# Two bf16 values as one 4-byte element: all transposes of a retention and mixing kernel on TensorE, none on the DMA

## Chip, cores and metric

One core of one Trainium2 chip. The metric is the device time of one execution in microseconds (us), as the median of several runs. "The span" is the length of one profiled execution; where the time and the span of the same run are both known, the time is in most runs about 1.7 us longer. "The clock" is the share of its full rate that TensorE was granted. A run more than 1.5% above the fastest of the same kernel is called slow; medians and ranges hold all runs, ratios the fast ones alone.

## The reference, cut to what matters

```python
# q, k, v: (4, 8, 768, 64) fp32;  attention with a decaying state
state = gamma * state + k_t (outer) v_t          # per head
y_t   = scale * q_t @ state
# x = y as (4, 768, 512); then the mixing layer
theta = x @ w_theta
y = w_tok_r @ (x * cos(theta)) + w_tok_i @ (x * sin(theta))   # over tokens
u = x + y
out = u + max(u @ w_ch, 0)
```

The kernel does it in chunks of 128 tokens: 24 chunks of attention, and 24 rows (blocks of 128 tokens) of the mixing layer. In each product of TensorE here the summed index lies on the partitions, so k and q of each chunk, the attention result x, the rows of u and the token weights must each be turned by 128x128 blocks in bf16.

## The kernel before

The parts that the change touches. `att_*` are the steps of a chunk, `moe_*` those of a row.

```python
N_DMA = (B - 1) * nT + 1     # chunks from 19 on are turned by DMA
M_DMA = (B - 2) * nT         # rows from 12 on are turned by DMA
...
def att_prep(n):
    kqb = work.tile([P, 2, dm], BF, name="kqb", bufs=5)
    kb, qb = kqb[:, 0, :], kqb[:, 1, :]          # k and q side by side
    ...                                          # GpSimd casts and scales into them
def att_T(n):
    kq_ps = psum.tile([P, 2 * NP, P], BF, name="kq_ps", tag="tr", bufs=2)
    for i, src in enumerate((s["kb"], s["qb"])):
        for j in range(NP):                      # 8 transposes of 2-byte elements
            nc.tensor.transpose(kq_ps[:, i * NP + j, :], src[:, j * P:(j + 1) * P], ident)
    nc.vector.tensor_copy(kqT, kq_ps)            # contiguous copy out of PSUM
def att_T_dma(n):
    nc.sync.dma_start_transpose(out=kqT, in_=s["kqb"].rearrange("p a d -> p (a d)"))
...
def moe_last(m):             # the last row, in two halves
    ...
    moe_U_dma(m - 1)
    prods(0)
    moe_O(m - 2)
    prods(1)
    flip(0)
    moe_O(m - 1)
    flip(1)
    ...
# one slot of the main loop, in TensorE's order (cut)
    if n is not None and nT < n < N_DMA:       att_T(n)
    ...
    if U_at.get(s_ - 1, 0) >= M_DMA:           moe_O(U_at[s_ - 1])   # DMA row: a slot later
    ...
    if U_at.get(s_, M_DMA) < M_DMA:            moe_U(U_at[s_])
    ...
    if 1 < U_at.get(s_, M_DMA) < M_DMA:        moe_O(U_at[s_])
```

## Time and profile before

| | before |
|---|---|
| time, first runs | 182.69 us (182.03 to 184.78, 3 runs) |
| time beside the later calls, medians | 182.41 to 183.72 us |
| span of the profiled run, clock | 181.8 us, 1.00 in nearly every slice |
| TensorE busy | 157.7 us, 87% |
| VectorE, ScalarE, GpSimd busy | 104.8, 74.7, 79.9 us |

First, two of the three kinds of DMA transposes, and the output of whole rows, in the list of DMA issues (what, engine, count, for the output the size, median microseconds from issue to landing):

```profile
uT<-u SPq DMA_TRANSPOSE x11, 2.4
kqT<-kqb SPq DMA_TRANSPOSE x5, 3.8
out_dram<-ot SPq DMA_DIRECT2D x23, 256.0 KB, 2.2
```

Issuing one takes SyncE 1.2 us (median of the 11 of u).

Second, the end of the chain of waits in order of time (start, length, what):

```profile
171.92 0.76 PE y_ps L348 x7
172.67 3.02 DMA uT<-u
...
175.73 0.39 PE o_ps L310
...
177.35 0.41 PE o_ps L374 x2
```

The last row's y products start at 171.92 us. The chain then leaves TensorE for the DMA transpose of row 22, whose landing releases the o products at 175.73 us; TensorE itself waited only 0.2 us for it. TensorE is done at 177.76 us, and the output has landed by 181.8.

### The profile page before, as it was taken

The numbers are of one execution on the slowest core, as the hardware profiler recorded it, in microseconds if no ns is written. First come the engines' busy times: TensorE is split into PE (matmuls) and PEld (weight loads), VectorE is DVE, ScalarE is ACT, GpSimd is POOL, SyncE is SP. The second block draws the span as 40 slices with busy tenths as digits, with TensorE's granted clock in tenths as the row PEclk, the third lists the DMA queues.
The fourth block names the chain that finished last, engine by engine and source line by source line (L and its number), as shares of the span: only waits on it lengthen the run. The fifth ranks groups of instructions, "written<-read, shape, count | busy, mean of one in ns | idle before, by whom it ended". The sixth has DMA issues, their size and how long they took to land.

```text
span 181.8 us, 3528 instructions
## 1 busy us (share of the span) xinstructions
PE 157.7 (87%) x1367; PEld 90.7 (50%) x1392; DVE 104.8 (58%) x146; ACT 74.7 (41%) x140; POOL 79.9 (44%) x104
## 2 busy tenths in 40 slices
PE   0567987897764999999999999999999999999991
PEld 0344655553542655656565565455545544444560
DVE  1264794716822777878676877765645744434442
ACT  4053764821429535647554363356345332200010
POOL 4648677869075768865777847250000000000000
PEclk9999999999999999999999999999999999999997
DMA  6999999999998999999999989984483333334433
GB/s 128 222 316 218 224 276 259 294 288 231 227 259 180 260 243 225 222 272 271 223 228 251 266 208 233 263 151 115 119 112 102 103 97 90 104 93 110 132 105 117
DMA packets 95265, 35.63 MB, mean 196 GB/s; under 512 B 89488, under 2 KB 89744, under 8 KB 95248
## 3 DMA queue, kind: packets, MB, share of 16 engines
q1 hardware_dynamic: 95104, 35.27, 86.4%
q8 instruction: 11, 0.18, 0.5%
q10 hardware_dynamic: 144, 0.13, 0.2%
q14 instruction: 6, 0.05, 0.1%
HBM read 25.69 MB, written 6.29 MB: 176 GB/s over the span
## 4 chain that ended last, share of the span: by engine, by line
PE 62%; SPq 18%; DMA 12%; issue 2%; POOL 2%; DVE 1%; DVEq 0%
PE y_ps L282 27%; SPq L80 15%; PE o_ps L310 11%; PE th_ps L253 8%; DMA kf<-in_k_dram 4%; DMA qf<-in_q_dram 3%; PE yT_ps L214 3%; DMA wtok<-in_moe_w_tok_r_dram 3%; PE at_ps L185 3%; PE kq_ps L165 3%; PE st_ps L222 2%; SPq L94 2%; DMA uT<-u 2%; PE yT_ps L203 2%; PE x_ps L250 1%
## 5 line engine op out<-in xcount | busy, mean ns | idle before, releaser
L282 PE MATMUL y_ps<-z,wti 128*128 128x512 bf16 x137 | 51.9, 379 | 1.6 <-ACT wti L332 0.9
L282 PE MATMUL y_ps<-z,wtr 128*128 128x512 bf16 x125 | 47.4, 379 | 0.7 <-DVE u L287 0.3
L189 DVE TENSOR_TENSOR at<-at_ps,mask 128x1024 bf16<-128x1024 f32 x24 | 29.3, 1220 | 8.9 <-PE at_ps L185 8.8
L258 ACT ACTIVATE cs<-th_ps,halfpi 128x512 bf16<-128x512 f32 x24 | 16.5, 688 | 38.0 <-PE th_ps L253 34.1
L154 POOL TENSOR_TENSOR kqb<-qf,qsc 128x512 bf16<-128x512 f32 x24 | 25.7, 1071 | 11.3 <-DMA qf<-in_q_dram 11.1
L156 POOL TENSOR_TENSOR vb<-vf,vsc 128x512 bf16<-128x512 f32 x24 | 25.9, 1081 | 7.0 <-DMA vf<-in_v_dram 5.8
L264 DVE TENSOR_TENSOR z<-cs,x_sb 128x1024 bf16<-128x1024 bf16 x24 | 19.6, 818 | 14.2 <-ACT cs L259 14.2
L168 DVE COPY kqT<-kq_ps 128x1024 bf16<-128x1024 bf16 x19 | 13.1, 691 | 24.6 <-PE kq_ps L165 24.4
L253 PE MATMUL th_ps<-wth,xT 128*128 128x512 bf16 x89 | 24.4, 387 | 2.4 <-DVE wth L395 1.9
L153 POOL CAST kqb<-kf 128x512 bf16<-128x512 f32 x24 | 16.0, 667 | 19.9 <-DMA kf<-in_k_dram 14.1
L310 PE MATMUL o_ps<-wch,uT 128*128 128x512 bf16 x88 | 23.1, 379 | 0.4 <-DMA uT<-u 0.2
L165 PE MATMUL kq_ps<-ident,kqb 128*128 128x128 bf16 x152 | 13.6, 234 | 11.1 <-POOL kqb L153 7.0
L287 DVE TENSOR_TENSOR u<-y_ps,x_sb 128x512 bf16<-128x512 f32 x23 | 15.8, 690 | 11.9 <-PE y_ps L282 11.9
L313 DVE SCALAR_TENSOR_TENSOR ot<-o_ps,u 128x512 f32<-128x512 f32 x23 | 15.9, 692 | 10.7 <-PE o_ps L310 10.7
L231 ACT CAST xT<-yT_ps 128x512 bf16<-128x512 f32 x24 | 14.1, 586 | 19.4 <-PE yT_ps L214 18.1
L282 PEld LDWEIGHTS <-wti 128*128 128x128 bf16 x138 | 13.5, 98 | 15.4 <-issue 1.9
L282 PEld LDWEIGHTS <-wtr 128*128 128x128 bf16 x138 | 13.5, 98 | 13.5
L165 PEld LDWEIGHTS <-kqb 128*128 128x128 bf16 x152 | 10.6, 104 | 16.5 <-POOL kqb L153 7.9
L259 ACT ACTIVATE cs<-th_ps,zerob 128x512 bf16<-128x512 f32 x24 | 16.3, 681 | 0.0
L236 ACT CAST stbd<-st_ps 64x256 bf16<-64x256 f32 x40 | 14.7, 366 | 0.5
L310 PEld LDWEIGHTS <-uT 128*128 128x128 bf16 x92 | 8.8, 98 | 10.3 <-DMA uT<-u 0.4
L253 PEld LDWEIGHTS <-xT 128*128 128x128 bf16 x96 | 8.8, 100 | 9.2 <-issue 2.6
(51 smaller groups left out, 147.3 us busy)
## 6 DMA issues: line engine op xcount, KB each, us to landing
kf<-in_k_dram SPq DMA_DIRECT2D x24, 256.0 KB, 4.9
qf<-in_q_dram SPq DMA_DIRECT2D x24, 256.0 KB, 5.0
vf<-in_v_dram SPq DMA_DIRECT2D x24, 256.0 KB, 5.3
out_dram<-ot SPq DMA_DIRECT2D x23, 256.0 KB, 2.2
wtok<-in_moe_w_tok_r_dram SPq DMA_DIRECT2D x6, 384.0 KB, 5.3
wtok<-in_moe_w_tok_i_dram SPq DMA_DIRECT2D x6, 384.0 KB, 5.9
w<-in_moe_w_theta_dram SPq DMA_DIRECT2D x1, 1024.0 KB, 6.7
w<-in_moe_w_ch_dram SPq DMA_DIRECT2D x1, 1024.0 KB, 7.8
```

Source lines behind the costliest of these rows:

```text
L80: nc.sync.dma_start(out=t, in_=src[b, :, c * P:(c + 1) * P, :].rearrange("h s d -> s h d"))
L153: nc.gpsimd.tensor_copy(kb.rearrange(r3, h=H), raw[n, "kf"])
L154: nc.gpsimd.tensor_mul(qb.rearrange(r3, h=H), raw[n, "qf"], _bcast_last(qsc[:, c], D))
L156: nc.gpsimd.tensor_mul(vb.rearrange(r3, h=H), raw[n, "vf"], _bcast_last(vsc[:, c], D))
L165: nc.tensor.transpose(kq_ps[:, i * NP + j, :], src[:, j * P:(j + 1) * P], ident)
L189: nc.vector.tensor_mul(at.rearrange("p a j t -> p (a j) t"), at_ps.rearrange("p a j t -> p (a j) t"), _bcast_mid(mask, H))
L253: nc.tensor.matmul(th_ps, s["xT"][:, j, :], wth[:, j, :], start=(j == 0), stop=(j == NP - 1))
L258: nc.scalar.activation(cs[:, 0, :], th_ps, AF.Sin, bias=halfpi, scale=1.0)
L259: nc.scalar.activation(cs[:, 1, :], th_ps, AF.Sin, bias=zerob, scale=1.0)
L264: nc.vector.tensor_mul(zs[b][:, c], st[n]["cs"], _bcast_mid(xs[b][:, c, :], 2))
L282: nc.tensor.matmul(y_ps, wT[r][:, s0, t0 * P:(t0 + 1) * P], zs[b][:, s0, r, :], start=(s0 == 0 and r == 0), stop=(s0 == nT - 1 and r == 1))
L310: nc.tensor.matmul(o_ps, mo[m]["uT"][:, j, :], wch[:, j, :], start=(j == 0), stop=(j == nD - 1))
```

## The change

The intent: a 4-byte element holds two bf16 values, so a transpose of 128x128 4-byte elements turns two blocks at once. With half the instructions, TensorE takes over all transposes, also those of the DMA. k and q are stored interleaved, and the copy of VectorE out of PSUM takes them apart with a step of two elements. For u and the token weights the pairs are left in, and the reader of the turned block (a weight load with a step of two) picks its half. For x, the theta products read the unturned block with a step of two, and the features of the turned one come out in another order; the weights of theta are put into that order too, and the last sum undoes it. The core of the diff (the same pattern for x, u and the token weights, and the reordered weights, are cut):

```diff
-    N_DMA = (B - 1) * nT + 1
-    M_DMA = (B - 2) * nT
...
-    ident = const.tile([P, P], BF)
+    ident = const.tile([P, P], FT)
...
-        kqb = work.tile([P, 2, dm], BF, name="kqb", bufs=5)
-        kb, qb = kqb[:, 0, :], kqb[:, 1, :]
+        kqb = work.tile([P, dm, 2], BF, name="kqb", bufs=5)
+        kb, qb = kqb[:, :, 0], kqb[:, :, 1]
...
+        kq_ps = psum.tile([P, NP, P], FT, name="kq_ps", tag="tr", bufs=2)
+        for j in range(NP):
+            nc.tensor.transpose(kq_ps[:, j, :],
+                                s["kqb"][:, j * P:(j + 1) * P, :].rearrange(
+                                    "p c i -> p (c i)").bitcast(FT), ident)
+        kqT = work.tile([P, 2, NP, P], BF, name="kqT", bufs=4)
+        nc.vector.tensor_copy(kqT.rearrange("p i j t -> p i (j t)"),
+                              kq_ps.rearrange("p j t -> p (j t)").bitcast(BF)
+                                  .rearrange("p (c i) -> p i c", i=2))
-    def att_T_dma(n):                      # and att_X_dma, moe_U_dma
...
     def moe_last(m):
-        moe_U_dma(m - 1)
+        moe_U(m - 1)
         prods(0)
         moe_O(m - 2)
...
-        if n is not None and nT < n < N_DMA:
+        if n is not None and n > nT:
             att_T(n)
...
-        if U_at.get(s_ - 1, 0) >= M_DMA:
-            moe_O(U_at[s_ - 1])
...
-        if 1 < U_at.get(s_, M_DMA) < M_DMA:
+        if U_at.get(s_, 0) > 1:
             moe_O(U_at[s_])
```

More of the change, by code (lines that the diff above doesn't have):

```diff
@@ L141 @@
     wch = const.tile([P, nD, dm], BF)
-    wT = [const.tile([P, nT, S], BF, name="wtr"), const.tile([P, nT, S], BF, name="wti")]
+    wT = [const.tile([P, nT, nT // 2, P, 2], BF, name="wtr"),
+          const.tile([P, nT, nT // 2, P, 2], BF, name="wti")]
     st = {}
@@ L161, in att_T @@
         s = st[n]
-        kq_ps = psum.tile([P, 2 * NP, P], BF, name="kq_ps", tag="tr", bufs=2)
-        for i, src in enumerate((s["kb"], s["qb"])):
-            for j in range(NP):
-                nc.tensor.transpose(kq_ps[:, i * NP + j, :],
-                                    src[:, j * P:(j + 1) * P], ident)
-        kqT = work.tile([P, 2 * NP, P], BF, name="kqT", bufs=4)
-        nc.vector.tensor_copy(kqT, kq_ps)
-        s["kqT"] = kqT
-    def att_T_dma(n):
-        s = st[n]
-        kqT = work.tile([P, 2 * NP, P], BF, name="kqT", bufs=4)
-        nc.sync.dma_start_transpose(
-            out=kqT, in_=s["kqb"].rearrange("p a d -> p (a d)"))
-        s["kqT"] = kqT
+        kq_ps = psum.tile([P, NP, P], FT, name="kq_ps", tag="tr", bufs=2)
[5 more added lines that the diff above has]
+        nc.vector.tensor_copy(kqT.rearrange("p i j t -> p i (j t)"),
+                              kq_ps.rearrange("p j t -> p (j t)").bitcast(BF).rearrange("p (c i) -> p i c", i=2))
+        s["kT"] = [kqT[:, 0, j, :] for j in range(NP)]
+        s["qT"] = [kqT[:, 1, j, :] for j in range(NP)]
     def att_A(n):
         s = st[n]
-        kqT = s["kqT"]
         at_ps = psum.tile([P, 2, NP, P], FT, name="at_ps", tag="at", bufs=1)
@@ L184, in att_A @@
                 rows = slice(par * D, (par + 1) * D)
-                nc.tensor.matmul(at_ps[:, par, j, :], kqT[rows, j, :],
-                                 kqT[rows, NP + j, :], start=(j == 0),
+                nc.tensor.matmul(at_ps[:, par, j, :], s["kT"][j][rows],
+                                 s["qT"][j][rows], start=(j == 0),
                                  stop=(j == NP - 1), skip_group_check=True)
@@ L203, in att_Yinter @@
                 nc.tensor.matmul(s["yT_ps"][:, j, :], stbd[c % 2][:, j, :],
-                                 s["kqT"][:, NP + j, :], start=(j == 0), stop=False,
+                                 s["qT"][j], start=(j == 0), stop=False,
                                  skip_group_check=True)
@@ L229, in att_Y @@
             zs[b] = big.tile([P, nT, 2, dm], BF, name="z")
-        xT = work.tile([P, NP, P], BF, name="xT", bufs=3)
-        nc.scalar.copy(xT, yT_ps)
+        xT = work.tile([P, NP // 2, P, 2], BF, name="xT", bufs=3)
+        nc.scalar.copy(xT.rearrange("p a t b -> p a b t"),
+                       yT_ps.rearrange("p (b a) t -> p a b t", b=2))
         s["xT"] = xT
@@ L236, in att_Y @@
                 nc.scalar.copy(stbd[(c + 1) % 2][sl, :, sl], st_ps[b][sl, :, sl])
-    def att_X_dma(n):
-        b, c = divmod(n, nT)
-        nc.sync.dma_start_transpose(
-            out=xs[b][:, c, :].rearrange("p (j e) -> p j e", j=NP),
-            in_=st[n]["xT"].rearrange("p j t -> p (j t)"))
     def att_X(n):
@@ L246, in att_X @@
         s = st[n]
-        if n < N_DMA:
-            x_ps = psum.tile([P, NP, P], BF, name="x_ps", tag="tr", bufs=2)
-            for j in range(NP):
-                nc.tensor.transpose(x_ps[:, j, :], s["xT"][:, j, :], ident)
+        x_ps = psum.tile([P, NP // 2, P], FT, name="x_ps", tag="tr", bufs=2)
+        for a in range(NP // 2):
+            nc.tensor.transpose(x_ps[:, a, :],
+                                s["xT"][:, a].rearrange(
+                                    "p t i -> p (t i)").bitcast(FT), ident)
         th_ps = psum.tile([P, dm], FT, name="th_ps", tag="acc", bufs=2)
         for j in range(NP):
-            nc.tensor.matmul(th_ps, s["xT"][:, j, :], wth[:, j, :], start=(j == 0),
-                             stop=(j == NP - 1))
-        if n < N_DMA:
-            nc.vector.tensor_copy(xs[b][:, c, :], x_ps.rearrange("p j e -> p (j e)"))
+            nc.tensor.matmul(th_ps, s["xT"][:, j % 2, :, j // 2], wth[:, j, :],
+                             start=(j == 0), stop=(j == NP - 1))
+        nc.vector.tensor_copy(xs[b][:, c, :],
+                              x_ps.rearrange("p a e -> p (a e)").bitcast(BF))
         cs = work.tile([P, 2, dm], BF, name="cs", bufs=2)
@@ L281, in moe_M @@
             for r in range(2):
-                nc.tensor.matmul(y_ps, wT[r][:, s0, t0 * P:(t0 + 1) * P],
+                nc.tensor.matmul(y_ps, wT[r][:, t0, s0 % (nT // 2), :, s0 // (nT // 2)],
                                  zs[b][:, s0, r, :], start=(s0 == 0 and r == 0),
@@ L290, in moe_U @@
     def moe_U(m):
-        u_ps = psum.tile([P, nD, P], BF, name="u_ps", tag="tr", bufs=2)
-        for j in range(nD):
-            nc.tensor.transpose(u_ps[:, j, :], mo[m]["u"][:, j * P:(j + 1) * P], ident)
-        uT = work.tile([P, nD, P], BF, name="uT", bufs=3)
-        nc.scalar.copy(uT, u_ps)
-        mo[m]["uT"] = uT
-    def moe_U_dma(m):
-        uT = work.tile([P, nD, P], BF, name="uT", bufs=3)
-        nc.sync.dma_start_transpose(out=uT, in_=mo[m]["u"])
-        mo[m]["uT"] = uT
+        u_ps = psum.tile([P, nD // 2, P], FT, name="u_ps", tag="tr", bufs=2)
+        for a in range(nD // 2):
+            nc.tensor.transpose(u_ps[:, a, :],
+                                mo[m]["u"][:, 2 * a * P:2 * (a + 1) * P].bitcast(FT),
+                                ident)
+        uT = work.tile([P, nD // 2, P, 2], BF, name="uT", bufs=3)
+        nc.scalar.copy(uT.rearrange("p a t i -> p (a t i)"),
+                       u_ps.rearrange("p a t -> p (a t)").bitcast(BF))
+        mo[m]["uT"] = [uT[:, j % 2, :, j // 2] for j in range(nD)]
     def moe_O(m):
         b, t0 = divmod(m, nT)
-        if m >= M_DMA:
-            o_ps = psum.tile([P, dm], FT, name="o_ps", tag="tr", bufs=2)
-        else:
-            o_ps = psum.tile([P, dm], FT, name="o_ps", tag="acc", bufs=2)
+        o_ps = psum.tile([P, dm], FT, name="o_ps", tag="acc", bufs=2)
         for j in range(nD):
-            nc.tensor.matmul(o_ps, mo[m]["uT"][:, j, :], wch[:, j, :], start=(j == 0),
+            nc.tensor.matmul(o_ps, mo[m]["uT"][j], wch[:, j, :], start=(j == 0),
                              stop=(j == nD - 1))
         ot = work.tile([P, dm], FT, name="ot", bufs=4)
-        nc.vector.scalar_tensor_tensor(ot, o_ps, 0.0, mo[m]["u"], ALU.max, ALU.add)
+        nc.vector.scalar_tensor_tensor(
+            ot.rearrange("p (b r) -> p b r", b=2),
+            o_ps.rearrange("p (b r) -> p b r", b=2), 0.0,
+            mo[m]["u"].rearrange("p (r b) -> p b r", b=2),
+            ALU.max, ALU.add)
         nc.sync.dma_start(out=out[b, t0 * P:(t0 + 1) * P, :], in_=ot)
@@ L320, in w_cast @@
             row = work.tile([P, S], BF, name="wrow", bufs=3)
-            nc.gpsimd.tensor_copy(row, wdma[r, t0])
+            nc.gpsimd.tensor_copy(
+                row.rearrange("p (i b) -> p b i", b=2),
+                wdma[r, t0].rearrange("p (b i) -> p b i", b=2))
             wrow[r, t0] = row
@@ L325, in w_tok @@
         for r in range(2):
-            w_ps = psum.tile([P, nT, P], BF, name="w_ps", tag="tr", bufs=2)
-            for s0 in range(nT):
-                nc.tensor.transpose(w_ps[:, s0, :],
-                                    wrow[r, t0][:, s0 * P:(s0 + 1) * P], ident)
-            dst = wT[r][:, :, t0 * P:(t0 + 1) * P]
+            w_ps = psum.tile([P, nT // 2, P], FT, name="w_ps", tag="tr", bufs=2)
+            for a in range(nT // 2):
+                nc.tensor.transpose(
+                    w_ps[:, a, :],
+                    wrow[r, t0][:, 2 * a * P:2 * (a + 1) * P].bitcast(FT), ident)
+            dst = wT[r][:, t0].rearrange("p a t b -> p (a t b)")
+            src = w_ps.rearrange("p a t -> p (a t)").bitcast(BF)
             if r:
-                nc.scalar.copy(dst, w_ps)
+                nc.scalar.copy(dst, src)
             else:
-                nc.vector.tensor_copy(dst, w_ps)
+                nc.vector.tensor_copy(dst, src)
     def moe_last(m):
@@ L342, in moe_last @@
         u = work.tile([P, dm], BF, name="u", bufs=4)
-        uT = work.tile([P, nD, P], BF, name="uT", bufs=3)
+        uT = work.tile([P, nD // 2, P, 2], BF, name="uT", bufs=3)
         def prods(e):
@@ L347, in prods @@
                 for r in range(2):
-                    nc.tensor.matmul(y_ps[e], wT[r][:, s0, t0 * P:(t0 + 1) * P],
+                    nc.tensor.matmul(y_ps[e], wT[r][:, t0, s0 % (nT // 2), :, s0 // (nT // 2)],
                                      zs[b][:, s0, r, e * hw:(e + 1) * hw],
@@ L355, in flip @@
         def flip(e):
-            u_ps = psum.tile([P, 2, P], BF, name="u_ps", tag="tr", bufs=2)
-            for j in range(2):
-                jj = 2 * e + j
-                nc.tensor.transpose(u_ps[:, j, :], u[:, jj * P:(jj + 1) * P], ident)
-            nc.scalar.copy(uT[:, 2 * e:2 * e + 2, :], u_ps)
-        moe_U_dma(m - 1)
+            u_ps = psum.tile([P, P], FT, name="u_ps", tag="tr", bufs=2)
+            nc.tensor.transpose(u_ps, u[:, e * hw:(e + 1) * hw].bitcast(FT), ident)
+            nc.scalar.copy(uT[:, e].rearrange("p t i -> p (t i)"), u_ps.bitcast(BF))
+        moe_U(m - 1)
         prods(0)
@@ L370, in moe_last @@
                 psum.tile([P, hw], FT, name="o_ps", tag="acc", bufs=2)]
-        for js in ((0, 1), (2, 3)):
+        for js in ((0, 2), (1, 3)):
             for e in range(2):
                 for j in js:
-                    nc.tensor.matmul(o_ps[e], uT[:, j, :],
+                    nc.tensor.matmul(o_ps[e], uT[:, j % 2, :, j // 2],
                                      wch[:, j, e * hw:(e + 1) * hw], start=(j == 0),
@@ L378, in moe_last @@
             ot = work.tile([P, hw], FT, name="oh", bufs=2)
-            nc.vector.scalar_tensor_tensor(ot, o_ps[e], 0.0, u[:, e * hw:(e + 1) * hw],
-                                           ALU.max, ALU.add)
+            nc.vector.scalar_tensor_tensor(
+                ot, o_ps[e], 0.0, u.rearrange("p (r b) -> p b r", b=2)[:, e],
+                ALU.max, ALU.add)
             (nc.sync, nc.scalar)[e].dma_start(
@@ L394 @@
         if n == 1:
-            nc.vector.tensor_copy(wth, wdma["th"])
+            nc.vector.tensor_copy(
+                wth[:, :nD // 2].rearrange("p d (r b) -> p d b r", b=2),
+                wdma["th"][:, :nD // 2].rearrange("p d (b r) -> p d b r", b=2))
+            nc.scalar.copy(
+                wth[:, nD // 2:].rearrange("p d (r b) -> p d b r", b=2),
+                wdma["th"][:, nD // 2:].rearrange("p d (b r) -> p d b r", b=2))
         if n > 0:
@@ L445 @@
             load_chunk(n + 5)
-        if U_at.get(s_, 0) >= M_DMA:
-            moe_U_dma(U_at[s_])
-        if n is not None and nT < n < N_DMA:
+        if n is not None and n > nT:
             att_T(n)
@@ L458 @@
             w_cast(3 + s_ // 2)
-        if s_ + 1 in n_of and n_of[s_ + 1] < N_DMA:
+        if s_ + 1 in n_of:
             att_prep(n_of[s_ + 1])
-        if s_ + 2 in n_of and n_of[s_ + 2] >= N_DMA:
-            att_prep(n_of[s_ + 2])
-            att_T_dma(n_of[s_ + 2])
         if s_ in (1, 3, 5):
             w_tok(3 + s_ // 2)
-        if U_at.get(s_ - 1, 0) >= M_DMA:
-            moe_O(U_at[s_ - 1])
         if s_ - 1 in n_of:
             att_Yinter(n_of[s_ - 1])
-        if U_at.get(s_, M_DMA) < M_DMA:
+        if s_ in U_at:
             moe_U(U_at[s_])
@@ L475 @@
             att_Y(n_of[s_ - 1])
-            if n_of[s_ - 1] >= N_DMA:
-                att_X_dma(n_of[s_ - 1])
         if s_ == 2:
```

## The prediction

> **What bounds the kernel now.** I read the page first (slices, chain), then the table of windows, the chain in order of time, and the groups by form. The slices of the page show two stages:
>
> ```profile
> PE   0567987897764999999999999999999999999991
> DMA  6999999999998999999999989984483333334433
> q1 hardware_dynamic: 95104, 35.27, 86.4%
> PE 62%; SPq 18%; DMA 12%; issue 2%; POOL 2%; DVE 1%; DVEq 0%
> ```
>
> In the first 13 slices (to about 58 us) the DMA engines are full and TensorE is not; from there to the end TensorE is at 9 tenths in every slice. The chain splits in the same place: 30% of the span is DMA and its queue, all of it at the start, and 62% is TensorE. In order of time it crosses over here, and then runs through TensorE slot by slot:
>
> ```profile
> 51.51 6.18 DMA qf<-in_q_dram
> 57.76 1.05 POOL kqb L154
> 58.86 0.41 PE kq_ps L165 x4
> 59.29 0.04 DVE kqT L168
> 59.33 0.57 issue
> 59.90 0.68 DVE z L264
> 60.59 0.69 DVE u L287
> 61.28 0.47 DVE wtr L334
> 61.80 0.38 PE u_ps L293 x4
> ...
> 98.42 0.45 PE kq_ps L165 x8
> 98.87 1.29 PE y_ps L282 x6
> 100.16 0.22 PE yT_ps L203 x4
> 100.39 0.22 PE u_ps L293 x4
> ```
>
> The reader is to see that a load's landing releases the kq transposes at 58.86 us, that after a short stretch on VectorE everything on the chain is TensorE back to back, and that eight kq transposes cost 0.45 us, four u transposes 0.22 us: 56 ns each from start to start. (The 219 to 234 ns in the groups is the length of one, with its pipeline; what a packed stage pays is the 56 ns.) One full slot, 98.42 to 104.86 us, is 6.44 us, and the pieces of the chain sum to it: kq 0.45, y 2.53, carried y 0.22, u 0.22, at 0.33, yT 0.34, state 0.33, o 0.86, x 0.22, theta 0.86, with about 0.06 between. So after 58.9 us, time is the sum of what TensorE is given. Loads are not behind there: the chunk whose kq transposes start at 98.4 us was ready on GpSimd at 89 us, though the one used at 66.0 us was ready at 62.5 us, so early on there are only some 3.5 us to spare.
>
> The rows that the sum needs:
>
> ```profile
> L165 PE MATMUL kq_ps<-ident,kqb 128*128 128x128 bf16 x152 | 13.6, 234 | 11.1 <-POOL kqb L153 7.0 <-POOL kqb L154 4.1
> L165 PEld LDWEIGHTS <-kqb 128*128 128x128 bf16 x152 | 10.6, 104 | 16.5 <-POOL kqb L153 7.9 <-POOL kqb L154 5.0 <-issue 0.5
> L168 DVE COPY kqT<-kq_ps 128x1024 bf16<-128x1024 bf16 x19 | 13.1, 691 | 24.6 <-PE kq_ps L165 24.4
> L189 DVE TENSOR_TENSOR at<-at_ps,mask 128x1024 bf16<-128x1024 f32 x24 | 29.3, 1220 | 8.9 <-PE at_ps L185 8.8
> ```
>
> **What the Trainium skill says.** "TensorE: Matmul & The Clock Gate", Terms (xbus row), has a transpose mode that is "4× faster for FP32". If a 4-byte matmul otherwise takes four passes, the 128 columns of a 4-byte transpose stream as fast as 2-byte ones. The same page, Weight-path perf modes, says fast weight load is on for 128 weights whose type is not FP32, and its section LDWEIGHTS gives columns divided by 1.2, so 107 ns for 128. In this kernel the data to be turned is the weight operand (the second row above), so that path is used by every transpose. The trace agrees for 2 bytes (56 ns apart, so weights load inside that) and has not one 4-byte operand on TensorE: the cost of the new transpose is in no row. "VectorE: DVE Perf Modes", What auto-detection actually checks, gives the mode with two elements per cycle only to 16-bit operands of step 1. The trace agrees: 1024 bf16 contiguous from PSUM take 691 ns, 1024 elements in fp32 take 1220 ns. "GPSIMD Engine Reference", Performance pitfalls, warns of reads with a step over 8 bytes; the new steps are 4 bytes and on the write side, which no row shows.
>
> **The change part by part**, after 58.9 us, where TensorE's sum is the time.
>
> Removed. Transposes of 2 bytes on TensorE: kq of 10 chunks x 8 = 80, x of 12 chunks x 4 = 48, u of 10 rows x 4 and the last row's 4 = 44, token weights 2 x 12 = 24. Sum 196, at 0.0556 us: 10.9 us. Removed too are 21 DMA transposes (5 kqT, 5 x, 11 uT). These cost the chain almost nothing: TensorE waited for uT 0.22 us in all, in the tail.
>
> Added. The remaining work with half the instructions, but also the share that the DMA did: kq of 15 chunks x 4 = 60, x of 17 x 2 = 34, u of 21 rows x 2 and the last's 2 = 44, weights 2 x 6 = 12. Sum 150, each costing t. So the TensorE sum changes by 150 t - 10.9 us. It breaks even at t = 73 ns. A normal slot goes from 6.44 to 6.44 - 0.89 + 8t; a late slot, whose transposes were on the DMA, gets 8t on top.
>
> What t is, is the whole question:
> - 56 ns, if the stream is one column per cycle and the weights load behind the previous stream: -2.5 us.
> - 107 ns, if the 4-byte weight load without the fast path is the limit: 150 x 0.107 = 16.1, so +5.2 us.
> - 160 ns, if load and stream no longer overlap (107 + 53): +13.1 us.
> - 213 ns, if four passes are made after all (4 x 53): +21.1 us.
>
> Moved. The kq copy must read with step 2, so it drops to one element per cycle: 691 to about 1220 ns, the time of the at product. That is +0.53 us per slot and five more copies, plus five x copies of 0.41 us. Per slot VectorE goes from about 4.5 us (ot 0.69, x 0.41, kqT 0.69, z 0.82, at 1.22, u 0.69) to 5.0 of 6.4 us: beside TensorE, not on the path. It is on the path in one place, the VectorE stretch at 59.3 to 61.8 us: +0.5 us. ScalarE gets 11 more uT copies of 586 ns; it is idle there.
>
> The tail. The row before the last was turned by DMA while TensorE went on with the last row. Now its transposes stand first in TensorE's order and wait for the VectorE sum u (0.69 us plus 0.2 us of latency): about +0.9 us, less the 0.2 us of the wait removed, +0.7 us.
>
> The first stage: the loads and their queue bound it, and they do not change. TensorE has some 10 us idle between 10 and 57 us, so its transposes there are free at t up to about 213 ns (78 instead of 156).
>
> Strided weights (theta, o, y, state products): loads of 98 ns beside streams of 216 ns, hidden; I count nothing.
>
> Sum: 182.7 + 150 t - 10.9 + 1.2, that is 181 at 56 ns, 189 at 107, 196 at 160, 204 at 213.
>
> **The rivals.**
> (a) TensorE's sum falls and the kernel gets slightly faster. For: half the transposes, the page's phrase on FP32. Against: even then it is 2.5 us less the 1.2 us of new waits. Result 180 to 182.
> (b) The 4-byte weight load becomes the bound of each transpose, and the DMA's share comes back onto the full engine. For: the page excludes FP32 from the fast load, and the late slots were relieved on purpose. Against: weight loads of 128 rows x 64 columns, which by "TensorEngine Tiling (Array Packing)", Restrictions, have no fast path either, take 109 ns here against 98, only 11 ns more, so a slow load may still hide. Result 188 to 197.
> (c) VectorE becomes the bound, with 5.0 us in slots that shrink to 6.0. For: its copies must come just before the at product. Against: over 1 us per slot is left, and in the slot at 105 us the copy would still end some 0.3 us before the product needs it. Result 1 to 3 us on top of (a).
> (d) The DMA was slowed by its transposes, and loads get faster without them. Against: the kq transposes are issued at 110 us and later, when the last loads are going out. Worth nothing.
>
> **Range and chances.** I give t near 56 ns 0.40, near 107 ns 0.32, and 160 ns or more 0.28. The middle of that is about 187 us, between the cases rather than in one. Eight in ten: 180 to 203. Faster by 2% needs 179.0 us or less, which even (a) misses: 0.05. Within 2% (up to 186.3 us) is (a) with or without (c): 0.42. Slower: 0.53.
>
> **What would show it.** Look for eight transposes per slot of 4-byte type: their start-to-start time is t, and the stretch after about 59 us should move by 150 t - 10.9 us. The kqT copy should read about 1220 ns. The chain should still cross from DMA to TensorE near 59 us, with the VectorE piece about 0.5 us longer. In the tail TensorE should wait about 0.9 us for u before the last row. The mean would be wrong if TensorE shows gaps in the normal slots (then (c)), if the crossing moves by more than 1 us (slower strided writes on GpSimd), or if the strided weight loads of the big products are longer than 216 ns.

## More of the kernel before

The prediction shows the slices, the chain across the border between the two stages, and the groups. Two more views matter later.

## The result

| | before | changed |
|---|---|---|
| time, same rounds | 182.74 us (182.03 to 184.78, 4 runs) | 187.69 us (187.02 to 188.88, 4 runs) |
| ratio | | 1.0275 (95%: 1.0205 to 1.0345), slower |
| span, clock of the profiled run | 181.8 us | 185.3 us, 1.00 |
| TensorE busy | 157.7 us | 164.4 us |
| VectorE, ScalarE, GpSimd busy | 104.8, 74.7, 79.9 us | 120.2, 84.7, 84.7 us |

A ratio is the mean time of one kernel's fast runs over that of the other's fast runs of the same rounds, so it is not quite the ratio of the medians. Both kernels give the right result.

The page of the changed kernel, slices and chain:

```profile
PE   0377887796897999999999999999999999999993
DMA  6999999999999999999999968111011011112114
PE 65%; SPq 21%; DMA 6%; ACT 2%; issue 2%; POOL 2%; DVE 0%; DVEq 0%
```

The shape is the same: loads bound the first 13 slices, TensorE is full from there on. The DMA is now nearly idle from slice 25 on, where it ran at 3 to 4 tenths before. That idle time buys nothing: the DMA had room there.

The groups for the kq transposes and their copy (line, engine, operation, shapes, count, busy us and mean ns, idle time before them), and the output's issues:

```profile
L163 PE MATMUL kq_ps<-ident,kqb 128*128 128x128 f32 x96 | 16.1, 294 | 7.1 <-POOL kqb L153 7.1
L163 PEld LDWEIGHTS kq_ps<-ident,kqb 128*128 128x128 f32 x96 | 12.3, 150 | 12.3 <-POOL kqb L153 8.9
L167 DVE COPY kqT<-kq_ps 128x1024 bf16<-128x1024 bf16 x24 | 29.3, 1223 | 22.3 <-PE kq_ps L163 22.2
out_dram<-ot SPq DMA_DIRECT2D x24, 256.0 KB, 2.0
```

The record of a 4-byte weight load is 150 ns long, against 104 for a 2-byte one; the copy went from 691 to 1223 ns, as the prediction had it. The last line is a surprise: 24 whole-row outputs, where the page of the kernel before has 23 (shown above). The chain at the border, in a full slot, and in the tail:

```profile
59.20 0.70 ACT wti L324
...
59.95 0.44 PE u_ps L282 x2
...
96.63 0.44 PE kq_ps L163 x4
97.07 1.29 PE y_ps L271 x6
...
98.58 0.22 PE u_ps L282 x2
...
175.25 0.86 PE o_ps L294 x4
176.11 0.36 PE u_ps L282 x2
176.47 1.31 PE y_ps L340 x12
...
181.50 0.41 PE o_ps L364 x2
```

Four 4-byte transposes of k and q take 0.44 us, so **110 ns each**. Eight 2-byte ones took 0.45 us, two 4-byte ones of u take 0.22 us, and four 2-byte ones took the same. A 4-byte transpose costs what the two that it replaces cost. The slot is 6.42 us long (96.63 to 103.05), against 6.44.

I split both profiled runs at two points of the chain: at the start of the u transposes where it enters TensorE for good (near 60 us), and at the start of the last row's y products.

| stretch | before | changed | difference |
|---|---|---|---|
| start to the u transposes near 60 us | 61.80 | 59.95 | -1.85 |
| from there to the last row's y | 110.12 | 116.52 | +6.40 |
| last row's y to TensorE's last product's end | 5.84 | 5.44 | -0.40 |
| from there to the end of the span | 4.04 | 3.39 | -0.65 |
| span | 181.80 | 185.30 | +3.50 |

The first line moves by itself: in the repeat of the changed kernel the same point was at 60.82 us, and in the other variants whose first stage holds the same TensorE work, pairs or not, it was between 60.36 and 62.11 (63.19 in one with a dip of the clock there). It follows how the loads land, and one profile says little about it. The medians differ by 5.0 us and the spans by 3.5, because one profile of each is one draw: 187.02 was the fastest of the changed kernel's four runs, and a span of 181.8 before belongs, with the 1.7 us above, to a run of about 183.5 us (an estimate). So what has to be explained is the second to fourth lines, together +5.35 us. Below, "the second stage" is these three together: 120.0 us before, 125.35 us changed.

**A row made twice.** Row 21 is the third from the end. In the kernel before it belongs to the DMA rows, whose `moe_O` comes one slot later; there is no such slot for it, so `moe_last` makes it as `moe_O(m - 2)`. In the changed kernel the slot itself makes it (`if U_at.get(s_, 0) > 1`), and `moe_last` makes it again. That is the 24th output; the bytes written to memory rose from 6.29 to 6.55 MB, one row of 0.26 MB, and the weight loads of o from 92 to 96. One o product of four matmuls is 0.86 us on TensorE. The prediction had not seen it.

### The profile page after: what moved, and what is told of

Its sections match the earlier page's. It is cut to its first block, busy times and chain, and to the rows that moved or that the text cites. A ratio compares the mean times of both kernels' runs of the same rounds, so it can differ in the third digit from the quotient of the medians.

```text
span 185.3 us, 3289 instructions
## 1 busy us (share of the span) xinstructions
PE 164.4 (89%) x1250; PEld 96.6 (52%) x1272; DVE 120.2 (65%) x157; ACT 84.7 (46%) x152; POOL 84.7 (46%) x104
## 3 DMA queue, kind: packets, MB, share of 16 engines
q1 hardware_dynamic: 81264, 32.12, 74.7%
HBM read 25.69 MB, written 6.55 MB: 174 GB/s over the span
## 4 chain that ended last, share of the span: by engine, by line
PE 65%; SPq 21%; DMA 6%; ACT 2%; issue 2%; POOL 2%; DVE 0%; DVEq 0%
PE y_ps L271 26%; SPq L78 18%; PE o_ps L294 11%; PE th_ps L242 8%; PE kq_ps L163 3%; DMA vf<-in_v_dram 3%; PE yT_ps L207 3%; DMA wtok<-in_moe_w_tok_r_dram 3%; PE u_ps L282 3%; PE at_ps L178 3%; PE st_ps L215 2%; PE x_ps L237 2%; SPq L92 2%; POOL wrow L309 2%; PE yT_ps L196 2%
## 5 line engine op out<-in xcount | busy, mean ns | idle before, releaser
L167 DVE COPY kqT<-kq_ps 128x1024 bf16<-128x1024 bf16 x24 | 29.3, 1223 | 22.3 <-PE kq_ps L163 22.2
L182 DVE TENSOR_TENSOR at<-at_ps,mask 128x1024 bf16<-128x1024 f32 x24 | 29.3, 1221 | 7.0 <-PE at_ps L178 6.7
L152 POOL CAST kqb<-kf 128x512 bf16<-128x512 f32 x24 | 19.1, 798 | 19.2 <-DMA kf<-in_k_dram 10.6
L286 ACT COPY uT<-u_ps 128x512 bf16<-128x512 bf16 x23 | 13.5, 585 | 27.9 <-PE u_ps L282 27.9
L294 PE MATMUL o_ps<-wch,uT 128*128 128x512 bf16 x94 | 24.1, 379 | 0.1
L224 ACT CAST xT<-yT_ps 128x512 bf16<-128x512 f32 x24 | 17.7, 739 | 13.9 <-PE yT_ps L207 12.3
L163 PE MATMUL kq_ps<-ident,kqb 128*128 128x128 f32 x96 | 16.1, 294 | 7.1 <-POOL kqb L153 7.1
L253 DVE TENSOR_TENSOR z<-cs,x_sb 128x1024 bf16<-128x1024 bf16 x24 | 18.1, 752 | 6.3 <-ACT cs L248 6.3
L297 DVE SCALAR_TENSOR_TENSOR ot<-o_ps,u 128x512 f32<-128x512 f32 x24 | 16.6, 692 | 4.7 <-PE o_ps L294 4.7
L163 PEld LDWEIGHTS kq_ps<-ident,kqb 128*128 128x128 f32 x96 | 12.3, 150 | 12.3 <-POOL kqb L153 8.9
L309 POOL CAST wrow<-wtok 128x768 bf16<-128x768 f32 x12 | 13.0, 1098 | 4.4 <-DMA wtok<-in_moe_w_tok_r_dram 2.0
```

The costliest lines, as they stand in the source:

```text
L152: nc.gpsimd.tensor_copy(kb.rearrange(r3, h=H), raw[n, "kf"])
L163: nc.tensor.transpose(kq_ps[:, j, :], s["kqb"][:, j * P:(j + 1) * P, :].rearrange("p c i -> p (c i)").bitcast(FT), ident)
L167: nc.vector.tensor_copy(kqT.rearrange("p i j t -> p i (j t)"), kq_ps.rearrange("p j t -> p (j t)").bitcast(BF).rearrange("p (c i) -> p i c ...
L182: nc.vector.tensor_mul(at.rearrange("p a j t -> p (a j) t"), at_ps.rearrange("p a j t -> p (a j) t"), _bcast_mid(mask, H))
L224: nc.scalar.copy(xT.rearrange("p a t b -> p a b t"), yT_ps.rearrange("p (b a) t -> p a b t", b=2))
L253: nc.vector.tensor_mul(zs[b][:, c], st[n]["cs"], _bcast_mid(xs[b][:, c, :], 2))
```

## The experiments

My theory (A) after the result: the pairs neither win nor lose on TensorE, and the loss is the DMA's share of the transposes put back on a full TensorE, 104 two-byte transposes at 56 ns, 5.8 us. The rivals: (B) the pairs themselves cost something, through the strided copy, the strided writes or the strided weights; (C) the DMA's transposes had hidden costs whose removal gives something back. All edits of "before" or "changed" are against the kernels above.

### Only the share moved, no pairs

```diff
 # against before
-    N_DMA = (B - 1) * nT + 1
-    M_DMA = (B - 2) * nT
+    N_DMA = NCH
+    M_DMA = NCH
-        moe_U_dma(m - 1)
+        moe_U(m - 1)
```

> The kernel before, with its transposes still 2 bytes wide, but all of them on TensorE and none on the DMA. Theory A (the loss is the work that the DMA did and that is now on a full TensorE; a 4-byte transpose costs 110 ns, twice 55, so pairs neither win nor lose there): the DMA did 5 kq x 8 + 5 x x 4 + 11 u x 4 = 104 transposes of 2 bytes, at 55.6 ns that is +5.8 us on the kernel before, so about 188.0 us, the same as the changed kernel (187.7) within 1 us. Rival B (the pairs themselves cost: the slower kq copy on VectorE, the 4-byte weight load, the strided operands): this kernel would keep clear of them and be near 185 us or less. Rival C (the DMA transposes were worth nothing or harmed): 182.7 or less. Also looked at: when the chain crosses from the loads to TensorE (61.8 us before at the u transposes of the slot, 59.95 us in the changed kernel).

Measured: 189.37 us (188.37 to 190.92), ratio 1.0334 (1.0242 to 1.0427), result correct. From the u transposes near 60 us (60.81) to the end of the span: 125.4 us; the changed kernel has 125.35. One slot:

```profile
97.44 0.45 PE kq_ps L165 x8
```

This kernel has no 4-byte transpose and no strided copy, and it loses as much as the changed one: the second stage is equally long, and the ratios overlap (1.0334 against 1.0275). The time itself is above the 188.0 expected, in a sitting where the kernel before took 183.72. (It makes row 21 twice as well, with 24 outputs, for the same reason.) The loss comes from moving the DMA's share, as (A) has it; what is left of (C) stands under "The tail" below.

### Only the pairs of k and q, the DMA's share kept

```diff
 # against before; ident4 is an fp32 identity
-        kqb = work.tile([P, 2, dm], BF, name="kqb", bufs=5)
-        kb, qb = kqb[:, 0, :], kqb[:, 1, :]
+        if n < N_DMA:
+            kqb = work.tile([P, dm, 2], BF, name="kqb", bufs=5)
+            kb, qb = kqb[:, :, 0], kqb[:, :, 1]
+        else:  # as before
 # att_T with 4 pair transposes and the copy with step 2, as in the change
```

> The kernel before, DMA transposes kept, but k and q of the first 19 chunks turned as 4-byte pairs with the copy that takes them apart. Theory A: 4 x 110 ns in place of 8 x 55.6 ns per chunk, so nothing on TensorE; kq copy 1.22 us in place of 0.69, beside TensorE but for the one VectorE stretch near 60 us: +0 to +0.7 us, so 182.5 to 183.5 us. Rival B (the copy on VectorE costs in each slot): ten packed slots x 0.3 to 0.5 us, so 185.5 to 187.5 us. If the crossing is earlier here as in the changed kernel, it belongs to the kq part.

Measured: 184.29 us median of four, of which the profiled run (199.76 us at a mean clock of 0.87) was slow and one more (185.68) was no fast run; ratio of the fast runs 0.9952 (0.9867 to 1.0037). Its profile can't be used.

> The kernel before with only k and q as pairs, again, because its profile fell in the slow state. Theory A: ratio 0.99 to 1.01, second stage 120.0 us plus 0 to 0.5 (kq 4 x 110 ns for 8 x 56 ns). Rival B (the slower copy on VectorE costs in each slot): second stage 123 us or more.

Measured: 182.04 us (181.44 to 182.85, 6 runs), ratio 0.9967 (0.9915 to 1.0020), clock 1.00. The copy took 1221 ns. From 60.56 us to the end: 119.64 us, against 120.0 before.

```profile
97.22 0.44 PE kq_ps L170 x4
```

The pairs alone, with their slow copy and strided writes, change nothing that these runs can see. (B) falls for k and q; the x, u and token pairs were not tried alone, but the stretch of the all-TensorE variant without any pairs (125.4 against 125.35) leaves little room for a cost of theirs there (the repeat of the changed kernel, further down, has 125.8, so some 0.5 us of it can't be seen).

### The changed kernel with a contiguous copy

The copy is contiguous, and TensorE reads k and q with a step of two instead.

```diff
 # against changed
-        kqT = work.tile([P, 2, NP, P], BF, name="kqT", bufs=4)
-        nc.vector.tensor_copy(kqT.rearrange("p i j t -> p i (j t)"), ...)
-        s["kT"] = [kqT[:, 0, j, :] for j in range(NP)]
-        s["qT"] = [kqT[:, 1, j, :] for j in range(NP)]
+        kqT = work.tile([P, NP, P, 2], BF, name="kqT", bufs=4)
+        nc.vector.tensor_copy(kqT.rearrange("p j t i -> p (j t i)"), ...)
+        s["kT"] = [kqT[:, j, :, 0] for j in range(NP)]
+        s["qT"] = [kqT[:, j, :, 1] for j in range(NP)]
```

> The changed kernel with the kq copy left contiguous; TensorE reads k and q from the pairs with step 2 instead (result stays right). Copy should fall from 1223 to about 690 ns, 24 times, 12.8 us less on VectorE. Theory A: VectorE is beside the path, so the time falls by 0 to 0.7 us (187.0 to 187.7), unless the moving operand of step 2 streams slower, which the start-to-start time of the at product (41 ns) would show. Rival B (the copy is the loss): falls by 3 us or more, to 184.5 or less.

Measured: 189.92 us (188.24 to 191.58, the last a slow run), ratio 1.0310 (1.0222 to 1.0399), correct. The time is above the 187.0 to 187.7 expected, in the same sitting as the last; the ratio overlaps with that of the changed kernel.

```profile
L167 DVE COPY kqT<-kq_ps 128x1024 bf16<-128x1024 bf16 x24 | 16.6, 691 | 26.5 <-PE kq_ps L163 26.4
```

The copy is back at 691 ns, 12.7 us of VectorE's time are gone, and the second stage is 125.5 us, as long as in the changed kernel (125.35). The products that now read with a step of two, eight in 0.33 to 0.34 us, are no slower. So the longer copy is beside the path. In the list of waits, TensorE waited 2.8 us for kqT in the changed kernel and 0.8 us here, and the time did not follow; VectorE is not the bound.

### Each k and q transpose made twice

```diff
 # against changed
-        for j in range(NP):
+        for j in [*range(NP), *range(NP)]:
```

> The changed kernel with every kq transpose issued twice into the same place (result right). Theory A (after some 60 us the time is TensorE's sum, and a 4-byte transpose costs 110 ns): 15 chunks x 4 x 0.110 = +6.6 us in that stage, nothing in the first, so 194.3 us. Rival (transposes hide behind VectorE or the loads): less than +3 us.

Measured: 197.45 us (196.98 to 198.81), ratio 1.0763 (1.0692 to 1.0834), correct.

```profile
96.34 0.87 PE kq_ps L163 x8
```

The second stage went from 125.35 to 131.5 us: +6.15. Fourteen chunks pass there, so 14 x 4 x 0.110 = 6.16: 110 ns is what one transpose puts on the time. But the whole is about 9.0 us longer (1.0763 less 1.0275, times 183.7), so the ten chunks of the first stage, with 4.4 us more of transposes, cost between 1 and 5 us too (each ratio is good to about 1.3 us), and the point near 60 us moved to 63.89. (Its profile also has a dip of the clock to 7 tenths near 20 us, so the 63.89 is not the transposes' alone; the ratio rests on four runs. Three of them have a mean clock of 0.99, but the slowest, 198.81 us, has 0.999.) The first stage has not the free room that the prediction gave it. Whether this room matters for the change itself is another question: there the first stage's transposes are half as many at twice the price.

### What the 110 ns are made of

A transpose loads its data as weights (128 columns) and streams the identity. Here each one is cut into two of 64 data rows: 128 columns are still loaded, but only 64 columns are streamed. The result is wrong.

```diff
 # against changed
-            nc.tensor.transpose(kq_ps[:, j, :], s["kqb"][:, ...], ident)
+            for h in range(2):
+                nc.tensor.transpose(kq_ps[:, j, h * D:(h + 1) * D],
+                                    s["kqb"][:D, ...], ident[:D, :D])
```

> The changed kernel with each kq transpose replaced by two that read rows 0 to 63 only: same weight load of 128 columns of 4 bytes, but a stream of 64 columns in place of 128 (wrong result on purpose: rows 64 to 127 are never read). What sets the 110 ns: Theory L (the 4-byte weight load): each of the eight still takes 110 ns, 0.88 us per chunk, +6.6 us in the packed stage, some 194 us. Theory S (the stream of 4-byte columns): each takes about 55 ns, eight take 0.44 us as before, time unchanged. In between: load and stream do not overlap fully.

Measured, one look (span 195.3 us, clock 1.00, the state of a single run is not known):

```profile
L164 PEld LDWEIGHTS kq_ps<-ident,kqb 64*128 64x128 f32 x192 | 15.2, 151 | 16.9 <-POOL kqb L153 8.1
...
104.08 0.64 PE kq_ps L164 x8
104.72 1.40 PE y_ps L272 x6
```

Eight in 0.64 us: 80 ns each. (The following y took 0.11 us longer than its usual 1.29, once for each switch back to full rows.) Neither simple story holds: if the load alone set the pace, this would still be 110; if the stream alone did, in two passes, 55. In the same way with four of 32 rows, again wrong:

> The changed kernel with each kq transpose replaced by four that read rows 0 to 31 only: weight load of 128 columns of 4 bytes as before, stream of 32 columns (wrong result on purpose). Theory N (load and stream of a 4-byte transpose do not overlap, each at one column per clock: 53 + 53 + 3 = 110 ns for 128 rows, 53 + 27 = 80 ns for 64, which was measured): 53 + 13 = some 67 ns each, sixteen in 1.07 us. If the load alone were the floor at 80 ns: 1.28 us. If the stream sets it: 0.44 us.

```profile
106.97 1.10 PE kq_ps L164 x16
```

Sixteen in 1.10 us (span 209.1 us, clock 1.00): 69 ns each. For 128, 64 and 32 streamed columns it is 110, 80 and 69 ns. The 96 columns between first and last are worth 41 ns, 0.43 ns a column (0.47 from 128 to 64, 0.34 from 64 to 32), so 128 columns are worth about 55 ns and about 55 ns remain. The weight load's record does not shrink either (150, 151, 154 ns). So these three points fit a fixed part of about 55 ns plus a stream of about 55 ns, one after the other; with 2 bytes the whole is 56 ns, so whatever the load takes there is hidden behind the stream. It is a fit: rows loaded and columns streamed shrink together here, and no 2-byte transpose with fewer rows was run. That the fixed part is the load of the 128 columns is the likely reading, but not shown: no run here loads fewer columns of 4 bytes.

### The changed kernel again

> The changed kernel as it is, beside the kernel before on the same chip: a second measurement of the change and of how much the first stage moves by itself. Expected: ratio 1.025 to 1.035; from the u transposes of the slot near 60 us to the end 125.4 us again (125.35 in its first profile, 125.4 in the two-byte kernel without DMA transposes, 120.0 before), and the crossing itself anywhere from 59.9 to 62.2 us, as the loads fall.

Measured: 187.86 us (187.71 to 188.32, 6 runs), ratio 1.0281 (1.0226 to 1.0335), clock 0.997. The point near 60 us is at 60.82, from there to the end 125.8 us. The result stands.

### More of the transposes to the DMA

If the share on TensorE costs, moving more of it away should gain. Two more chunks and two more rows go to the DMA.

```diff
 # against before
-    N_DMA = (B - 1) * nT + 1
-    M_DMA = (B - 2) * nT
+    N_DMA = (B - 1) * nT - 1
+    M_DMA = (B - 2) * nT - 2
```

> The kernel before, with two more chunks and two more u rows turned by the DMA (from chunk 17, row 10). Theory A (what leaves TensorE after 60 us is won, as long as the DMA delivers in time): 2 x (8 + 4) + 2 x 4 = 32 transposes of 55.6 ns fewer, -1.8 us, ratio 0.990. Rival (the queue is still full of loads until some 115 us, so the transposes land late and TensorE waits for kqT): same or slower, with TensorE waits on the DMA in the profile.

Measured: 185.87 us (183.58 to 187.27, 6 runs, three of them slow), ratio of the fast runs 1.0091 (1.0015 to 1.0167): no gain, rather a small loss. The profile had a dip of the clock between 50 and 70 us (mean 0.98).

> The kernel with two more chunks and two more u rows on the DMA again, on whatever chip comes: whether the dip of the granted clock near 50 to 70 us (0.98 in the mean of every run) belongs to the kernel or to that sitting. If to the kernel: 0.98 again and ratio near 1.01. If not: ratio near 0.99.

Measured: 185.39 us (183.14 to 186.58, 4 runs, the upper two slow) beside 183.13 before. The early dip did not come back, but another stood behind 123 us. The chain there:

```profile
119.45 1.21 SPq L240
...
121.34 2.43 DMA uT<-u
...
123.82 1.04 PE o_ps L310 x4
```

TensorE waited 2.8 us, once, for the first DMA-turned row of u (in the kernel before it waited 0.2 us for uT in all). The chain shows why: on SyncE's queue its issue stands behind that of an x transpose (L240, 1.21 us), and ahead of that, in the part cut here, behind an issue of a kq transpose (L174, 0.92 us) that itself waited for GpSimd. In the slice after the idle time the granted clock fell to 6 tenths. The profile of the first sitting does not have this wait. The lists of waits, the first sitting above, this one below (us in all, times, longest):

```profile
PE o_ps L310 <- DMA uT<-u: 0.3, 1, 0.3
PE o_ps L310 <- DMA uT<-u: 2.8, 1, 2.8
```

There the time was lost at the border, in the dip of the clock; from the kq transposes of chunk 10 (68.74 us) to the end it took 114.3 us, against 115.8 before (66.00 to 181.8). So in this one profile, where the DMA delivered in time, the gain was there.

> The kernel before with kq as pairs (0.997 of its time by itself) and two more chunks and two more u rows turned by the DMA (worth 1.5 us from the kq transposes of chunk 10 to the end in the first such run, 114.3 against 115.8 us, but that run had a dip of the granted clock before it). Theory A: the gain shows if the dip does not come: 1.5 us, ratio 0.988. Rival (the dip belongs to the further DMA transposes): ratio 1.00 to 1.01, mean clock near 0.98 in all runs.

Measured: 184.85 us (181.53 to 186.04, 6 runs, four of them slow), ratio of the two fast runs 0.9965 (0.9882 to 1.0047). Its profile fell in the slow state, and I rest nothing on it but that the same wait is there (3.0 us, once). So in two of three profiles what leaves TensorE at this place comes back as a wait for a DMA that was issued late. One of the four slow runs had a clock of 0.998, so the spread of these variants may be this wait coming and going, and not the clock; that is not shown. That the fast runs of this variant are not slower than before, while those of the one without pairs are, is left open.

### The changed kernel without the second row 21

```diff
 # against changed
         prods(0)
-        moe_O(m - 2)
         prods(1)
```

> The changed kernel computes the last matmul of row 21 and writes it out twice, once at the end of its slot and again in the tail (its profile has 96 weight loads of that line for 92 before, and 24 whole-row writes for 23). This removes the second one, in the tail. Theory A (time is TensorE's sum to the end): four streams of 216 ns less, -0.86 us on 187.7: 186.8 us, ratio to before 1.022 to 1.024 where the changed kernel had 1.0275 and 1.0281. Rival (the tail is bound by the copies and sums of the last row): unchanged.

Measured: 187.32 us (186.91 to 188.12, 6 runs), ratio 1.0227 (1.0167 to 1.0287), "unclear" against the 2% of the verdict, correct, clock 0.997, 23 outputs again. The tail of its chain:

```profile
176.38 0.86 PE o_ps L294 x4
177.25 0.36 PE u_ps L282 x2
```

From the last row's y (177.60) to the end of TensorE's last product (182.18) it is 4.58 us, against 5.44 with the second making: 0.86 us less. The ratio fell by about half a per cent, as much as 0.86 us, but the intervals overlap; the profile shows it, the times only agree. No version that I ran is clearly faster than the kernel before; the one with only the k and q pairs is equal to it.

## Why the prediction was right or wrong

The result, 187.7 us, is close to the 187.0 of the prediction, inside its range, and the outcome is the one it gave most to. The reasons fit less well than the number.

- **The bound and the border.** Right. The second stage is the sum of TensorE's work in every variant: what is added there (6.15 us of transposes) comes out on the time.
- **The cost t of a 4-byte transpose.** The size of the middle case, 107, was right: 110 ns. Its reason was wrong. The prediction had a load of 107 ns hiding the stream, and as another case load and stream one after the other, at 160. By the fit above it is the second mechanism with about half the fixed part: some 55 ns and 55 ns. The number came right because the two errors cancel, which is luck.
- **150 t - 10.9.** Right: at 110 ns it gives +5.6 us. From the border to the last row's y I measured +6.40, of which 0.86 is row 21 made early; 5.5 is left.
- **The step that was missed: row 21.** The prediction took the changed kernel's o products for the same 24 rows. They are 25 (+0.86 us).
- **The tail, +0.7 us.** Wrong. TensorE should have waited 0.9 us for u. It waits about 0.14 (0.36 us for two transposes, against 0.22). The products of row 21 made early stand just there, from 175.25 to 176.11 us, and fill the wait. With the second making taken out, they still do (176.38 to 177.25). On the whole the tail got shorter. From the last row's y to TensorE's last product it went from 5.84 to 5.44 us (0.86 us of row 21 are in both), but the four other such profiles of kernels that still turn the row before the last by DMA have 5.44 or 5.45 us, so the 0.40 us belongs to this one profile of the kernel before. The end of the output came 0.65 us sooner after TensorE's last product, and this follows the DMA transposes: it is 4.03 to 4.06 us in all five profiles of kernels that have them (the one at clock 0.87 left out), with pairs of k and q or without, and 3.37 to 3.46 us in all eight of kernels that have none, with pairs or without. That much of (C) holds; what it is that ends later was not looked into.
- **VectorE at the border, +0.5 us.** The copy's 1223 ns were predicted, the effect on the border was not seen: the point moves by more than that from run to run, the chain passed through ScalarE this time, and the second stage is no shorter with the copy back at 691 ns. No gaps in the normal slots, so rival (c) is out. (The page that the prediction names for the copy's speed does not give two elements per cycle "only" to 16-bit operands of step 1: it has another such mode for a source and destination in SBUF. The copy reads PSUM, so the reading holds for it.)
- **"Free up to 213 ns" in the first stage.** Not borne out. Doubling the k and q transposes cost about 3 us there (1 to 5). It did no harm to the sum, since in the change itself the first stage's transposes cost TensorE the same as before.
- **Rival (b)** named what happened, the DMA's share back on a full engine, but gave it 188 to 197; it is just below. By the formula with 110 ns and the two terms of 1.2 us it should have been 189.5. The share itself is shown by the variant without pairs: 125.4 us, the same second stage.
- **Rival (d)**, a gain of the loads, is not seen: the loads still land 5.0 to 5.2 us after their issue, 4.9 to 5.3 before.
- **Two sums** of the prediction are 1 us low: its formula gives 197.0 at 160 ns, not 196, and 205.0 at 213 ns, not 204. With its own chances the mean is then at least 188.2 (0.40 x 181.4, 0.32 x 189.1, 0.28 x 197.0), not 187.
- **The centre** of 187 was an average over cases, none of which it described, so that 187.7 came out is partly luck. From the 189.5 of the formula at 110 ns the measured time is off by -1.8 us: +0.9 for row 21, -1.0 for the tail's waits (+0.7 expected, +0.14 and, in this profile, -0.40 found), -0.5 at the border and -0.65 at the last output; the other -0.5 is within the scatter of the times.

## What to carry to other kernels

Fewer instructions are no gain by themselves on an engine that is full: ask what one of the new ones costs from start to start in a packed stream, and multiply. Work that a half-idle DMA does beside a full TensorE is worth its whole TensorE time, but only as long as its issue comes early enough in the queue. And when a change rewrites the conditions of a schedule, count the outputs of both kernels: a row made twice gives a right result and can only be seen in the counts.

## What the Trainium skill lacked or had wrong

- "TensorE: Matmul & The Clock Gate", Weight-path perf modes and LDWEIGHTS: the page gives a load's time, columns divided by 1.2, 107 ns for 128, and no fast load for FP32; of a 4-byte transpose it has no time from start to start. Here a 2-byte transpose with its load is 56 ns, a 4-byte one 110 ns, 80 ns with 64 and 69 ns with 32 columns streamed: by a fit of these three a fixed part of about 55 ns that is not hidden, and not 107. That the load's time follows columns and not rows is borne out by its records: 150, 151 and 154 ns for 128, 64 and 32 rows.
- The same page, Terms, "4× faster for FP32": the stream agrees (about 55 ns for 128 columns by the fit, no four passes). What is lacking is that the whole transpose is twice as long as with 2 bytes, so that pairs of bf16 gain nothing on TensorE.
- The same page, Back-to-back issue gap: about 81 ns per load and matmul of 128 columns and 131 ns of 512 in a sustained stream. Here 56 ns (eight transposes in 0.45 us) and 215 ns (six y products in 1.29 us); the formula that the section gives for an isolated gap, N / 2.4 + 2.5, fits the stream better than its sustained figures do.
- "GPSIMD Engine Reference", Performance pitfalls: it has only reads, with steps over 8 bytes. Casts that write bf16 with a step of 4 bytes took longer here as well: that of k went from 667 to 798 ns, that of the token weights from 960 to 1098 (638 to 676 and 887 to 960 in other profiles without the step, 758 to 825 and 1049 to 1110 with it). The multiplication that writes q with the same step hardly moved, from 1071 to 1084.
- "ScalarE: Activation LUTs" has nothing on steps: the copy of x out of PSUM, 128x512 elements, went from 586 to 739 ns when it read blocks in another order and wrote with a step of 4 bytes.
- "DMA: Bandwidth & Descriptors", Issuing engines are not separate DMA queues, calls the time to initiate a DMA "usually small relative to the DMA itself". For these transposes the issue takes SyncE 1.2 us and the landing 2.4 us, and the order of the issues cost TensorE 2.8 us in one profile.
